# Returning Y by transposes instead of transfers, and a rearranged hand-over to the second stage

## The chip, the cores and the metric

The kernel runs on one core of a Trainium2 chip. Times are device microseconds (us) of that core. A core has TensorE (PE; its weight loads are shown as PEld), VectorE (DVE), ScalarE (ACT), GpSimd (POOL), SyncE (SP) and 16 DMA engines. "Clock" is the share of TensorE's full rate that was granted.

## The reference, cut to what matters

```python
# x: 8 x 3264 x 192; first a causal 7-tap convolution per head (8 heads), giving x again, then:
X = np.fft.rfft(x, axis=1)                     # only the first 64 modes are used
Yr = einsum('bmd,mde->bme', Xr, w_r) - einsum('bmd,mde->bme', Xi, w_i)
Yi = einsum('bmd,mde->bme', Xr, w_i) + einsum('bmd,mde->bme', Xi, w_r)
y = np.fft.irfft(Y, n=S, axis=1)
u = x + y
return u + np.maximum(u @ w_ch, 0.0)           # float32, 8 x 3264 x 192
```

The matrices w_r and w_i (64 of 192 x 192 each) have to be loaded whole. The kernel uses (x + y) @ w_ch = x @ w_ch + G (Y @ w_ch), where G is the inverse transform, so Y is needed in two layouts: transposed (`yeT`) as the weights for Y @ w_ch, and with the modes on the partitions (`zy`) as the moving operand of G Y.

## The kernel before

Modes are worked in 16 groups of four. The parts that matter (cuts marked):

```python
def mix(g):                      # Y of four modes; two groups share one PSUM tile
    ...                          # 12 products per group, waiting for wtiles[g]
    ymix = workp.tile([P, D], BF16, tag="ymix")
    nc.scalar.activation(out=ymix[:], in_=zt[:, 0:D], func=ACT.Copy, ...)
    nc.sync.dma_start(out=zy[16 * i:16 * i + 16, :, :], in_=ymix[:, :])
    return ymix

def mix_t(g, ymix):              # two transposes and a copy make yeT
    ...

for g in range(NGRP):
    m = mix(g)
    ...                          # load of weights for a later group, into a freed buffer
    for _ in range(TPER[g]):     # steps of transposing the x data
        t_next(...)
    if g in (11, 13, 14): prefill()   # x @ w_ch of a unit, ahead of Y
    ...
# hand-over: zw = Y @ w_ch (16 products), then the units
zw_part(0); zw_part(1)
for n in range(4): gz(n)         # z += G zw, then relu on ACT
prefill(); gy(0); gz(4); gy(1); prefill(); gy(2); gz(5); gy(3)   # gy: z += G Y, then VectorE add and store
# then the loop: two half-row tiles (64 rows) of two units run side by side
```

There are 108 units of 128 rows by two batches. A "unit" ends with VectorE's add; two adds make one store. A "bank" is one of the PSUM tiles in which TensorE sums its products. A form such as 64*128 in the lines below gives the rows and columns of the weights; products on 64 rows and products on 128 rows are in different tile modes. `zwps<-ident` are filler products (`keep_warm` in the kernel) whose results are not used.

## Time and profile before

| | before |
|---|---|
| median | 183.28 us (3 runs, 183.02 to 183.29) |
| span of the profiled run | 181.4 us |
| last weight packet / sixteenth mix | 108.77 / 109.36 us |
| P0, the first zw product | 111.07 us |
| P0 to the start of the last G zw product, called "the ramp" with the experiments | 62.84 us |

The last line is read from the instruction records: the first zwps product at 111.07, the last `z<-zw` product of the loop at 173.91 (some `z<-win` and `z<-zy` products follow it, until 175.47). The prediction below shows the page's slices, the chain and the windows. Two more views: first who waited for whom from 56 to 110 us; the columns are total wait, times, longest wait:

```profile
PE yp L454 <- DMA wt<-in_moe_w_i_dram: 4.0, 4, 1.4
...
PE yp L454 <- DMA fst<-in_moe_w_i_dram: 1.6, 1, 1.6
```

Those are the mixes waiting for their weights: 5.6 us in which TensorE could do other work. Then VectorE's timeline at the hand-over (start, length, what, idle before it and what ended that):

```profile
113.98 2.42 DVE L572 TENSOR_TENSOR t<-z,x_all 128x384 f32<-128x384 f32 x5 [0.64 <-issue]
116.63 0.56 DVE L572 TENSOR_TENSOR t<-z,x_all 128x384 f32<-128x384 f32 x1 [0.22 <-PE z L502]
118.73 6.28 DVE L572 TENSOR_TENSOR t<-z,x_all 128x384 f32<-128x384 f32 x11 [1.54 <-PE z L537]
```

VectorE stands idle for 1.54 us before its seventh add.

### The profile page before, as it was taken

The numbers are of one execution on the slowest core, as the hardware profiler recorded it, in microseconds if no ns is written. First come the engines' busy times: TensorE is split into PE (matmuls) and PEld (weight loads), VectorE is DVE, ScalarE is ACT, GpSimd is POOL, SyncE is SP. The second block draws the span as 40 slices with busy tenths as digits, with TensorE's granted clock in tenths as the row PEclk, the third lists the DMA queues.
The fourth block names the chain that finished last, engine by engine and source line by source line (L and its number), as shares of the span: only waits on it lengthen the run. The fifth ranks groups of instructions, "written<-read, shape, count | busy, mean of one in ns | idle before, by whom it ended". The sixth has DMA issues, their size and how long they took to land.

```text
span 181.4 us, 5402 instructions
## 1 busy us (share of the span) xinstructions
PE 147.8 (81%) x2115; PEld 128.9 (71%) x2115; DVE 127.8 (70%) x256; ACT 112.9 (62%) x189; POOL 48.8 (27%) x74
## 2 busy tenths in 40 slices
PE   0373579989889969894649977999999999999970
PEld 0242359978779959783538866699999999999940
DVE  5879986553544446974462554679999999999990
ACT  2353994555558617774444453588888888888850
POOL 7969332459322244432523100000000000000000
PEclk9999558999999999999985999999999999999997
DMA  2999999999999999999999990479999999999995
GB/s 60 247 191 191 192 192 191 193 190 192 193 192 193 204 206 207 206 208 210 203 206 207 207 178 11 150 238 306 345 358 353 349 324 366 348 341 328 326 353 188
DMA packets 66819, 42.37 MB, mean 234 GB/s; under 512 B 30218, under 2 KB 66794, under 8 KB 66794
## 3 DMA queue, kind: packets, MB, share of 16 engines
q0 software_dynamic: 36048, 19.75, 78.2%
q1 hardware_dynamic: 30746, 22.28, 37.5%
q8 instruction: 16, 0.26, 0.7%
q14 instruction: 9, 0.07, 0.1%
HBM read 40.31 MB, written 21.01 MB: 338 GB/s over the span
## 4 chain that ended last, share of the span: by engine, by line
DMA 54%; PE 38%; POOL 2%; issue 2%; DVE 1%; DVEq 0%; ACT 0%; POOLq 0%; ACTq 0%
DMA x_all<-in_x_dram 29%; PE z L520 19%; DMA wt<-in_moe_w_i_dram 19%; PE z L537 13%; DMA fst<-in_moe_w_i_dram 6%; PE tp L418 2%; POOL x_all L61 2%; PE z L502 1%; PE yp L454 1%; PE zwps L488 1%; DVE t L572 1%; PE z L510 0%; POOL wt L251 0%; DVEq L722 0%; ACT ymix L463 0%
## 5 line engine op out<-in xcount | busy, mean ns | idle before, releaser
L572 DVE TENSOR_TENSOR t<-z,x_all 128x384 f32<-128x384 f32 x108 | 59.4, 557 | 3.9 <-PE z L537 1.5
L542 ACT ACTIVATE z<-z 128x384 f32<-128x384 f32 x108 | 50.7, 476 | 11.6 <-PE z L520 1.7
L537 PE MATMUL z<-zy,gst 64*128 64x384 bf16 x204 | 46.1, 323 | 0.2
L520 PE MATMUL z<-zw,gst 64*128 64x384 bf16 x204 | 46.1, 323 | 0.0
L520 PE MATMUL z<-win,cTa 64*128 64x192 bf16 x375 | 40.9, 243 | 0.0
L267 ACT CAST x_all<-cp 122x864 bf16<-122x864 f32 (+2 forms) x34 | 28.7, 880 | 15.4 <-PE cp L260 15.2
L520 PEld LDWEIGHTS <-cTa 64*128 64x128 bf16 x450 | 34.9, 94 | 2.8
L260 PE MATMUL cp<-x_all,cband 128*128 128x192 bf16 (+2 forms) x192 | 25.9, 287 | 8.8 <-DVE x_all L269 4.6
L260 PEld LDWEIGHTS <-cband 128*128 128x128 bf16 x192 | 19.7, 109 | 12.7 <-issue 5.4
L61 POOL DMA_DIRECT2D x_all<-in_x_dram x23 | 22.0, 969 | 10.8 <-DMA x_all<-in_x_dram 8.5
L269 DVE CAST x_all<-cp 122x768 bf16<-122x768 f32 (+2 forms) x14 | 14.7, 1054 | 13.2 <-PE cp L260 13.2
L423 ACT COPY cTa<-tp 128x854 bf16<-128x854 bf16 (+1 forms) x16 | 14.1, 910 | 14.7 <-PE tp L418 14.7
L282 PE MATMUL xp<-x_all,fst 122*128 122x192 bf16 (+1 forms) x216 | 22.0, 251 | 0.9 <-DVE x_all L269 0.5
L282 PEld LDWEIGHTS <-fst 122*128 122x128 bf16 (+1 forms) x216 | 18.2, 99 | 2.1 <-DVE x_all L269 0.7
L520 PEld LDWEIGHTS <-gst 64*128 64x128 bf16 x204 | 18.9, 94 | 0.7 <-issue 0.7
L520 PE MATMUL z<-win,cTb 64*128 64x192 bf16 x135 | 19.2, 243 | 0.0
L422 DVE COPY cTa<-tp 128x854 bf16<-128x854 bf16 (+1 forms) x17 | 10.6, 623 | 10.8 <-PE tp L418 10.6
L520 PE MATMUL z<-wB,cTa 64*128 64x192 bf16 x75 | 18.2, 243 | 0.0
L537 PEld LDWEIGHTS <-gst 64*128 64x128 bf16 x204 | 16.1, 93 | 1.0 <-POOLq L554 0.9
L520 PEld LDWEIGHTS <-cTb 64*128 64x128 bf16 x162 | 14.4, 94 | 1.1
L418 PE MATMUL tp<-ident,x_all 122*128 122x122 bf16 x216 | 15.0, 228 | 0.0
L251 POOL DMA_DIRECT2D wt<-in_moe_w_r_dram x14 | 8.6, 612 | 20.2 <-PE yp L454 6.2
(98 smaller groups left out, 169.5 us busy)
## 6 DMA issues: line engine op xcount, KB each, us to landing
out_dram<-t SPq DMA_DIRECT2D x52, 384.0 KB, 4.1
wt<-in_moe_w_r_dram POOLq DMA_DIRECT2D x14, 288.0 KB, 11.4
wt<-in_moe_w_i_dram POOLq DMA_DIRECT2D x14, 288.0 KB, 11.6
x_all<-in_x_dram POOLq DMA_DIRECT2D x8, 432.0 KB, 12.3
x_all<-in_x_dram POOLq DMA_DIRECT2D x7, 480.0 KB, 13.0
x_all<-in_x_dram POOLq DMA_DIRECT2D x8, 384.0 KB, 14.4
x<-in_x_dram SPq DMA_DIRECT2D x1, 768.0 KB, 6.0
fst<-in_moe_w_r_dram POOLq DMA_DIRECT2D x2, 288.0 KB, 10.5
```

Of the source, the lines that this page charges most:

```text
L61: nc.gpsimd.dma_start(out=x_all[:, b, c0:c0 + n, :], in_=src)
L260: nc.tensor.matmul(cp[:, j, 0:GRP * n].rearrange("p (w e) -> p w e", w=n), cband[:, h, :], x_all[:, b, w0:w0 + n, GRP * h:GRP * h + GRP], ...
L267: nc.scalar.copy(out=dst, in_=srcv)
L269: nc.vector.tensor_copy(out=dst, in_=srcv)
L282: nc.tensor.matmul(xp[:, 0:D], fst[0:k, c, :], x_all[0:k, b, c, :], start=(u == FIRST[b] and c == w0), stop=(u == LAST[b] and c == w0 + n ...
L418: nc.tensor.transpose(tp[:, WIN * k:WIN * k + WIN], slot_lhsT(p, k0 + k), ident[0:WIN, 0:WIN])
L422: nc.vector.tensor_copy(out=got[0][0], in_=got[0][1])
L423: nc.scalar.copy(out=got[1][0], in_=got[1][1])
L520: return nc.tensor.matmul(o, lhsT, rhs, start=start, stop=stop, skip_group_check=True, tile_position=(lo, 0))
L537: return [lambda: nc.tensor.matmul(zp[:, 0:2 * D], gst[lo:hi, WIN * w:WIN * w + P], zwi[(h, 1, k)][lo:hi, :], start=False, stop=(r == 1), ...
L542: return nc.scalar.activation(out=zp[:, 0:2 * D], in_=zp[:, 0:2 * D], func=ACT.Relu)
L572: add = nc.vector.tensor_tensor(out=t[:, 2 * k:2 * k + 2, :], in0=zp[:, 0:2 * D].rearrange("p (i e) -> p i e", i=2), in1=x_all[:, 4 * h + ...
```

## The change

Its intent: take six of the eight zy transfers off DMA engines that are full in the weight phase, by transposing `yeT` back on TensorE; let DVE and ACT copy two banks side by side at the hand-over; do the x product of a fifth unit before Y is there; fill VectorE's hole. Cut to its core:

```diff
+    YPE = 6
-        nc.sync.dma_start(out=zy[16 * i:16 * i + 16, :, :], in_=ymix[:, :])
+        if i >= YPE:
+            nc.sync.dma_start(out=zy[16 * i:16 * i + 16, :, :], in_=ymix[:, :])
+    def y_back(half):
+        tp = pt.tile([P, 1024], BF16, tag="p", name="yb")
+        n = 16 * YPE
+        for i in range(4):
+            for e in range(2):
+                e0 = 64 * e
+                nc.tensor.transpose(tp[0:n, D * i + P * e:D * i + P + 64 * e],
+                                    yeT[e0:P, e, 4 * half + i:n * B:B], ident[e0:P, e0:P])
+        nc.vector.tensor_copy(out=zy[0:n, 4 * half:4 * half + 4, :],
+                              in_=tp[0:n, 0:4 * D].rearrange("p (b e) -> p b e", b=4))
 ...
-    TPER = (1, 2, 1, 2, 2, 2, 1, 1, 2, 1, 2, 1, 2, 1, 1)
+    TPER = (1, 2, 1, 2, 2, 2, 1, 2, 2, 2, 2, 1, 1, 1, 0)
 ...
-            if g in (11, 13, 14):
+            if g in (10, 11, 14):
                 prefill()
+            if g in (12, 13):
+                y_back(g - 12)
 ...                                   # and one prefill more at group 14
-    zw_part(0)
-    zw_part(1)
-    for n in range(4):
-        gz(n)
+    zw_mm(0, 0, zwps[0:2])            # one batch in each of two banks
+    zw_mm(0, 1, zwps[2:3])
+    gz(0)
+    zw_mm(1, 0, zwps[0:1])
+    gz(1)
+    gz(2)
+    gy(0)
+    gz(3)
+    gy(1)
+    gz(4)
+    zw_mm(1, 1, zwps[1:2])
 ...
-    N, NF = len(seq), 6
+    N, NF, NY = len(seq), 6, 8        # units 6 and 7: y product whole, not in halves
```

## The prediction

> **What bounds the kernel now.** I read the page's slices first, then the chain that ended last in order of time, then the windows, then the timelines of TensorE and VectorE around the hand-over. The page:
>
> ```profile
> span 181.4 us, 5402 instructions
> ...
> PE   0373579989889969894649977999999999999970
> ...
> PEclk9999558999999999999985999999999999999997
> DMA  2999999999999999999999990479999999999995
> ...
> zy<-ymix SPq DMA_DIRECT2D x8, 48.0 KB, 5.6
> ```
>
> There are two halves. In slices 2 to 24 the DMA row reads 9 while TensorE has holes; from slice 27 TensorE reads 9 without a break. The chain shows the hand-over between them:
>
> ```profile
> 99.78 9.54 DMA wt<-in_moe_w_i_dram
> 109.32 0.04 issue
> 109.36 0.51 PE yp L454 x12
> ...
> 110.72 0.30 DVE yeT L473
> 111.02 0.05 issue
> 111.07 1.54 PE zwps L488 x16
> ```
>
> So the last weight transfer sets when the sixteenth mix may start (109.36), and 1.71 us later the second-stage products (zwps) start at 111.07; I call that moment P0. The windows show the two bounds:
>
> ```profile
> 86.00:90.00 4.00, 2.60 (x54) 2.33 (x51) 1.32 (x3) 1.30 (x2) 1.90 (x4) 1.00 1.22 207
> ...
> 94.00:98.00 4.00, 3.54 (x41) 3.26 (x41) 1.15 (x2) 0.87 (x1) 1.22 (x2) 0.50 1.21 207
> ...
> 140.00:174.60 34.60, 34.60 (x601) 32.08 (x596) 33.70 (x61) 28.75 (x62) 0.00 (x0) 1.00 1.02 341
> ```
>
> The columns are stretch and length, busy time of PE, weight loads, DVE, ACT and POOL, granted clock, DMA share, GB/s. In the weight phase TensorE has over a microsecond to spare in four and the rate stays at 207 GB/s; in the last stage TensorE is busy for 34.60 of 34.60 us. VectorE's 33.70 looks as full, but its adds start 0.573 us apart there, and only 0.465 apart where they queue (114.46, 114.92, 115.38), so it follows TensorE. TensorE needs 0.573 us for a unit: 0.164 + 3 x 0.082 = 0.41 for the z products of two half-row tiles side by side, and 0.164 for the y products. The end is therefore P0, plus the ramp to the steady pattern, plus a fixed number of 0.573 us periods and a fixed tail.
>
> **What the Trainium skill says.** "DMA: Bandwidth & Descriptors", section "Issuing engines are not separate DMA queues": transfers issued by any engine run on the same 16 DMA engines and interleave. The trace agrees: from 64 to 104 us its packet records start 88.5 weight packets per half microsecond when no zy packet starts in it, and 68.9 when over 40 do. "PSUM — Partial Sum Buffer", "PSUM bank collisions raise a hardware error": guard by bank, not by address. The trace agrees that the kernel does so: the ACT copy of the other batch of one zwps bank waited for the DVE copy (1.78 us idle before it, released by DVE zw L492). "TensorEngine Tiling (Array Packing)", "Key Properties": a change of tiling mode drains TensorE. The timeline agrees, with about 0.1 us:
>
> ```profile
> 114.54 0.33 PE L502 MATMUL z<-zw,gst 128*128 128x384 bf16 x1
> 114.70 0.33 PE L502 MATMUL z<-zy,gst 128*128 128x384 bf16 x1
> 114.96 0.33 PE L520 MATMUL z<-zw,gst 64*128 64x384 bf16 x1
> ...
> 115.30 0.24 PE L520 MATMUL z<-wB,cTa 64*128 64x192 bf16 x1
> 115.47 0.34 PE L502 MATMUL z<-zy,gst 128*128 128x384 bf16 x1
> 115.74 0.33 PE L520 MATMUL z<-zw,gst 64*128 64x384 bf16 x1
> ```
>
> Two 384-column products of one mode start 0.16 apart; from 128 to 64 rows it is 0.26, from 64 back to 128 rows 0.17 against 0.08. "TensorE: Matmul & The Clock Gate", Part 1: TensorE is held at half clock after a window of little activity. The trace agrees that it happens (0.50 above, after the emptier stretch 82 to 94).
>
> **The change, part by part.**
>
> 1. Six zy transfers go. Each is 128 packets of 384 B (with 16 small ones for the semaphore). By the regression over those half microseconds one zy packet displaces 0.32 weight packets, so a transfer costs 128 x 0.32 = 41 packets at 177 per us, 0.23 us. The ends of the weight transfers say the same: 1.43 us apart undisturbed, 1.65 to 1.68 where a zy transfer falls between. All six lie before the last weight packet (108.77), and the queue never starved: at the issue of each of the last ten transfers between 4.0 and 5.2 were outstanding. Gain 6 x 0.23 = **1.4 us** of P0.
>
> 2. In return come 16 transposes and two copies of 96x768. Transposes of this kind start about 0.06 us apart at full clock, the like copy of 128x854 takes 0.60: 0.5 us of TensorE and 0.6 of VectorE in each of groups 12 and 13. The weight transfers come every 3.1 us, and a group there holds a mix (0.5), one transpose step of the x data (0.9) and these. TPER has 22 steps before and after, moved to groups 7 and 9, where TensorE waited 1.41 and 1.55 us ahead of the next mix for a transfer. Group 14 keeps no step. So this hides: **0**.
>
> 3. A fifth unit is prefilled before P0: four products of 0.082, **-0.33 us** after P0.
>
> 4. The second-stage weights. Before, all sixteen products run (1.38 us) and then the first z, so TensorE is full, with one wait of 0.14. After, eight run (0.72); the first batch pair sits in two banks, so DVE and ACT copy side by side. A copy starts 0.28 after the start of its last product and takes 0.36 or 0.32, and TensorE answers 0.08 later: first z at P0 + 0.99 instead of 1.38. But TensorE idles 0.27 for that, then 0.07 for the 0.55 copy of the other pair, then about 0.23 for the second relu (0.48 after its z has ended), since gy(1) comes right behind. About 0.57 of idling against 0.14: **+0.4 us**, and it eats the prefill's gain. What it buys is the first VectorE add 0.6 us earlier, and VectorE is not the bound.
>
> 5. Units 6 and 7 take their y whole. Work is unchanged (two halves side by side or one whole, 0.164; the pairing is one slot longer than its units in both). But each whole y in the loop changes mode twice: 4 x 0.1 = **+0.4 us**. It closes VectorE's hole of 1.54 us ahead of 118.73, which delays nothing on TensorE.
>
> Followed instruction by instruction, the loop's round 12 starts at P0 + 7.4 now and P0 + 7.9 changed; from there both are alike. Sum: -1.4 - 0.33 + 0.4 + 0.4 and roundings, that is -1.4 + 0.5 = **-0.9 us**, so 183.28 - 0.9 = 182.4.
>
> **Rivals.** (a) The transfers were hidden, and the weight phase ends when it did. For it: the DMA share of 1.21 is an overlap of packets, not a proof of a full engine, and the last transfer ended 2.19 us after the one before, so its tail depends on the slowest engine. Against: 1.43 against 1.66. Then only the ramp counts: 183.8. (b) The ramp is free: VectorE's earlier start or banks coming free earlier matter, and the mode changes hide behind waits. For it: the author wrote it to fill VectorE's hole. Against: no wait of TensorE on a bank from 118 on. Then 183.28 - 1.4 - 0.33 = 181.55. (c) TensorE becomes late for the last mix, through the transposes at half clock as in 94 to 100.7. Its slack before mix 15 is 0.62 now and the work of group 14 shrinks, but a half clock that falls on the ramp would cost up to 1.7 us: 183.5 or more. Busier groups 7 and 9 speak against it.
>
> **Range and chances.** The centre takes part 1 whole and the ramp as worked out. The ends come from (b), and from half of part 1 lost or a bad clock window: 181.3 to 183.5. Two per cent is 3.7 us, more than twice all gains together: 0.02 faster, 0.97 the same, 0.01 slower.
>
> **What would show it.** Right for part 1: the sixteenth mix starts near 107.9 to 108.1, and weight transfers end 1.43 apart up to the seventh zy. Part 2: no wait of that mix on a DVE or ACT copy. Part 4: P0 to the first 64-row product about 4.05 us, with TensorE gaps ahead of the first z and of gy(1). Part 5: about 0.1 extra on either side of four whole y products in the loop, and the adds continuous with no hole of 1.5 us, yet still 0.573 apart. Wrong if mix 15 still starts at 109, if the adds run closer than 0.573 apart, or if the clock row has a 5 between the hand-over and the end.

## The result, and the profile after

The changed kernel takes 185.80 us (median of 4 runs, 185.46 to 186.11) beside 183.22 (4 runs, the three above and one more): ratio 1.0142, 95% interval 1.0122 to 1.0162. It is **slower by 1.4%**, clear of noise, though "the same" in the classes of 2% that the chances of the prediction go by. A ratio here is the mean time of one kernel's fast runs over that of the other's fast runs of the same rounds, so it is not quite the ratio of the medians. Executions over 1.5% slower than the fastest of the same kernel are left out of the means. The page of the changed kernel:

```profile
span 184.0 us, 5415 instructions
...
PE   0363679979989878867777989999999999999980
...
PEclk9999559999999999999999756999999999999997
DMA  2999999999999999999999920377999999999996
```

Two things differ from before. The DMA row falls a little earlier, so the weight phase did get shorter. And the low stretch of the clock row has moved, from slices 21 and 22 to slices 23 to 25, onto the hand-over. The chain that ended last, in order of time (start, length, what):

```profile
99.84 0.85 PE tp L418 x14
100.69 2.28 PE yb L477 x8
102.97 0.41 PE yp L455 x12
103.38 1.36 PE tp L418 x14
104.75 2.52 PE yb L477 x8
107.30 0.35 DVE zy L479
108.10 0.71 PE yp L455 x9
108.81 2.03 PE z L525 x12
110.84 0.64 PE zwps L628 x6
111.48 0.64 PE yp L455 x9
```

Before, a weight transfer of 9.54 us stood at this place. Now TensorE's own work, but for one VectorE copy at 107.30, leads to the sixteenth mix (111.41 in the records), nearly four microseconds after the last weight packet (107.49). (zwps of L628 are the fillers; the second-stage products start at P0, now 113.47.) The two groups of eight transposes back (yb) take 2.3 and 2.5 us, not 0.5. The windows name the second part; the first line is the kernel before, the other two the changed one:

```profile
104.00:108.00 4.00, 3.00 (x60) 2.74 (x53) 2.96 (x7) 1.98 (x4) 0.00 (x0) 1.00 1.16 200
104.00:108.00 4.00, 3.59 (x18) 2.73 (x16) 1.31 (x3) 0.87 (x1) 0.00 (x0) 0.50 0.86 150
108.00:112.00 4.00, 3.90 (x42) 3.06 (x41) 0.05 (x1) 0.00 (x0) 0.00 (x0) 0.50 0.00 0
```

The clock of the changed kernel was 0.50 for both stretches; by the clock records from 103.5 to 113.8, a length of 10.24 us. In 104 to 108 TensorE counts as 3.59 us busy with 18 matmuls; before it did 60 in 3.00 us. VectorE afterwards:

```profile
119.22 0.56 DVE L587 TENSOR_TENSOR t<-z,x_all 128x384 f32<-128x384 f32 x1 [0.22 <-PE z L517]
120.83 0.56 DVE L587 TENSOR_TENSOR t<-z,x_all 128x384 f32<-128x384 f32 x1 [1.05 <-PE z L517]
121.62 0.56 DVE L587 TENSOR_TENSOR t<-z,x_all 128x384 f32<-128x384 f32 x1 [0.23 <-PE z L517]
122.90 2.28 DVE L587 TENSOR_TENSOR t<-z,x_all 128x384 f32<-128x384 f32 x4 [0.72 <-PE z L552]
```

The single hole of 1.54 us became three of 1.05, 0.23 and 0.72. The adds then go on 0.573 us apart as before.

### The profile page after: what moved, and what is told of

The parts are those of the page before. It is cut to its first block, busy times and chain, and to the rows that moved or that the text cites. A ratio compares the mean times of both kernels' runs of the same rounds, so it can differ in the third digit from the quotient of the medians.

```text
span 184.0 us, 5415 instructions
## 1 busy us (share of the span) xinstructions
PE 152.4 (83%) x2129; PEld 131.4 (71%) x2129; DVE 127.7 (69%) x258; ACT 112.9 (61%) x188; POOL 49.1 (27%) x74
## 4 chain that ended last, share of the span: by engine, by line
DMA 47%; PE 43%; POOL 3%; issue 2%; DVE 2%; ACT 0%; DVEq 0%; POOLq 0%
DMA x_all<-in_x_dram 30%; PE z L535 19%; DMA wt<-in_moe_w_i_dram 18%; PE z L552 13%; PE yb L477 3%; POOL x_all L61 3%; PE tp L418 2%; PE yp L455 2%; PE z L517 1%; PE z L525 1%; PE zwps L628 1%; DVE t L587 1%; PE zwps L503 1%; POOL wt L251 0%; DVE yeT L487 0%
## 5 line engine op out<-in xcount | busy, mean ns | idle before, releaser
L552 PE MATMUL z<-zy,gst 64*128 64x384 bf16 x200 | 45.2, 323 | 0.2
L260 PE MATMUL cp<-x_all,cband 128*128 128x192 bf16 (+2 forms) x192 | 24.7, 277 | 8.7 <-DVE x_all L312 4.6
L260 PEld LDWEIGHTS <-cband 128*128 128x128 bf16 x192 | 18.8, 106 | 12.2 <-DVE x_all L312 5.5
L535 PEld LDWEIGHTS <-gst 64*128 64x128 bf16 x204 | 18.7, 94 | 1.0 <-issue 1.0
L552 PEld LDWEIGHTS <-gst 64*128 64x128 bf16 x200 | 15.8, 93 | 1.0 <-POOLq L569 0.9
L418 PE MATMUL tp<-ident,x_all 122*128 122x122 bf16 x216 | 13.6, 217 | 0.0
```

The lines of the kernel that those rows point to most:

```text
L260: nc.tensor.matmul(cp[:, j, 0:GRP * n].rearrange("p (w e) -> p w e", w=n), cband[:, h, :], x_all[:, b, w0:w0 + n, GRP * h:GRP * h + GRP], ...
L418: nc.tensor.transpose(tp[:, WIN * k:WIN * k + WIN], slot_lhsT(p, k0 + k), ident[0:WIN, 0:WIN])
L535: return nc.tensor.matmul(o, lhsT, rhs, start=start, stop=stop, skip_group_check=True, tile_position=(lo, 0))
L552: return [lambda: nc.tensor.matmul(zp[:, 0:2 * D], gst[lo:hi, WIN * w:WIN * w + P], zwi[(h, 1, k)][lo:hi, :], start=False, stop=(r == 1), ...
```

## The experiments

Where did the expected gain go? The weights did come earlier, but TensorE was no longer ready for them. Theory A: switching between 128-row and 64-row tiles at every one of the 16 transposes. Rivals: the stride of the weight reads (B), the moved transposes and prefills (C), a weight load of fewer than 128 columns (D, formed after the first runs); and for the size of the loss, the half clock (E). Eleven kernels ran, all correct.

**1. All transposes in one mode** (`e1_one_mode`), the changed kernel with

```diff
-                nc.tensor.transpose(tp[0:n, D * i + P * e:...], yeT[e0:P, e, ...], ident[e0:P, e0:P])
+                nc.tensor.transpose(tp[0:n, D * i + 64 * e:D * i + P + 64 * e],
+                                    yeT[:, e, 4 * half + i:n * B:B], ident[:, :])
```

> The changed kernel with all 16 transposes back in the full 128-row mode (the second of each pair also redoes 64 columns that the first wrote, with the same values). Theory A (what made the change slow is that each of the 16 transposes switches between 128-row and 64-row tiles and then starts 0.29 to 0.34 us after its forerunner): they start 0.06 to 0.1 us apart here, each group of eight takes under 0.8 us instead of 2.4 to 2.65, the sixteenth mix is released by its weight transfer near 108.1 us, no half clock falls on 104 to 114 us, and the time falls by 2.5 to 3.5 us to 182.3 to 183.3. Theory B (the transposes are slow because their weights are read with a stride of 8 elements): they stay near 0.3 us apart and the time stays at 185.8.

Measured: 182.09 us, ratio 0.9928 to before (0.9904 to 0.9952). TensorE's timeline:

```profile
100.45 1.57 PE L476 MATMUL yb<-ident,yeT 128*96 128x128 bf16 x8
...
103.21 1.57 PE L476 MATMUL yb<-ident,yeT 128*96 128x128 bf16 x8
...
107.95 0.48 PE L455 MATMUL yp<-wt,xt 128*32 128x192 bf16 x12 [0.41 <-DMA wt<-in_moe_w_i_dram]
...
109.67 0.47 PE L502 MATMUL zwps<-win,yeT 128*128 128x192 bf16 x3 [0.23 <-DVE yeT L486]
```

The sixteenth mix waits for its weights again, at 107.95, and no half clock falls near it. So the time falls as theory A says, 0.2 us below its range even. But the starts are 0.176 us apart, not the 0.06 to 0.1 expected: the mode is only part of a transpose's cost, and something else makes these transposes slow.

**2. Four of a kind, then the other four** (`e2_grouped`), the two `for` lines of the transposes exchanged.

> The same 16 transposes as in the changed kernel, 128 and 64 rows, but four of one kind and then four of the other, so one switch within a group of eight instead of seven. Theory A: each group of eight takes about 1 us (six starts of 0.06 to 0.1 and one or two switches of 0.3), the time is within 0.5 us of e1. Theory B, or a theory that 64-row transposes are slow by themselves: 64-row ones stay 0.3 apart and the time is over 184.5.

Measured: 183.37, with two runs at 184.2 and 184.4 and two at 181.7 and 182.5; ratio 0.999 (0.9938 to 1.0043). The 64-row transposes start 0.18 apart like the 128-row ones, so they are not slow by themselves, and the one switch in a group costs 0.27 to 0.31 from start to start. The profile happened to be of the slower sort, with half clock from 102.2 to 112.4: transposes hardly slower than in run 1 and a P0 2.4 us later than in run 1 all the same:

```profile
104.15 1.73 PE L477 MATMUL yb<-ident,yeT 128*96 128x128 bf16 x8
...
112.09 0.99 PE L503 MATMUL zwps<-win,yeT 128*128 128x192 bf16 x8
```

It is a miss for the time expected, and the first sign that the half clock is a cause of its own.

**3. No transposes back** (`e3_no_yback`), the changed kernel with YPE = 0 and no y_back.

> The changed kernel with all eight zy transfers by DMA and no transposes back: the prefill, the bank split, the whole y products and the moved transposes alone. Theory A with the ramp as predicted (0.5 to 0.7 us longer than before, because of waits and mode switches): sixteenth mix near 109.3 us as before, time 183.6 to 184.0. Rival (the ramp costs nothing): 182.9 to 183.3. Rival C (the moved transposes and prefill make TensorE late and cause the half clock, not the transposes back): sixteenth mix near 111 us, time over 185.

Measured: 184.57, ratio 1.0063 (1.0036 to 1.0089), somewhat more than expected. From P0 to the last z product it takes 63.35 us against 62.84 before: the ramp costs the 0.51 that was predicted. P0 itself came 0.49 later than before (111.56), with the last weight packet 0.57 later (109.34) and half clock from 106.2 to 109.6; why the packets were later isn't settled. The sixteenth mix started at 109.86, not at 111, so rival C is out as the main cause.

**4. The Y part alone, as in the change** (`e4_yback_alone`), the kernel before with YPE, y_back and the new TPER.

> The kernel before with the Y part alone (48 modes by the transposes of the changed kernel, alternating in mode, and the moved transposes of the x data), with the ramp of before. Theory A: the sixteenth mix is late by 2 to 2.5 us, half clock near 104 to 114 us, time about 185.2. Rival C: if the prefill schedule is what makes TensorE late, the time is about 182.

Measured: 185.60, ratio 1.0102 (1.0059 to 1.0145); sixteenth mix at 112.23, half clock from 101.9 to 112.1, ramp 62.84 as before. The Y part alone brings nearly the whole loss. One of its four runs took 183.81.

**5. The Y part alone, in one mode** (`e5_one_mode_alone`), run 4 with the diff of run 1.

> The kernel before with the Y part alone, its 16 transposes all in 128-row mode. Theory A (the zy transfers cost 1.3 to 1.4 us of the weight phase; the ramp of the change costs 0.5): the transposes start 0.18 us apart as in the one-mode run, the sixteenth mix is released by its weights near 108 us, the hand-over takes as long as before (62.8 us from the first second-stage product to the last z product), time 181.6 to 181.9. Rival (the ramp of the change costs nothing on the whole): 182.1 as in the one-mode run.

Measured: 181.37, ratio 0.9912 (0.9895 to 0.9928). P0 at 109.65 instead of 111.07, the last weight packet at 107.53 instead of 108.77, ramp 62.84. The six transfers were worth 1.2 to 1.4 us, as predicted; the time came 0.2 us below the range expected.

**6. One mode, units 6 and 7 in halves** (`e6_no_whole_y`), run 1 with NY = 6.

> The one-mode run with no whole y product in the loop beyond those of the kernel before (units 6 and 7 in halves). Theory A: four mode switches less, 0.1 us each: 0.4 us faster than the one-mode run, 181.6 to 181.8, and VectorE's hole of about 1.5 us before its seventh add is back. Rival (filling VectorE's hole pays): equal to the one-mode run or slower, 182.1 or more.

Measured: 181.29, ratio 0.9904 (0.9886 to 0.9922). The ramp is 62.93 instead of 63.36, so the two whole y products cost 0.43, four switches of 0.1 each. The time came 0.3 us below the range expected. VectorE's timeline has its hole back, at no cost to the end:

```profile
117.34 8.00 DVE L586 TENSOR_TENSOR t<-z,x_all 128x384 f32<-128x384 f32 x14 [1.54 <-PE z L551]
```

**7. One mode, loads of 128 columns** (`e7_wide_weights`), run 1 with the last 32 columns read and not used (their place is set to zero early on):

```diff
-                                    yeT[:, e, 4 * half + i:n * B:B], ident[:, :])
+                                    yeT[:, e, 4 * half + i:P * B:B], ident[:, :])
```

> The one-mode run with the transposes back reading 128 columns instead of 96 (the last 32 are not used). Theory D (a weight load of under 128 columns is slow, 0.25 to 0.27 us, and that is why the one-mode transposes still start 0.176 us apart): loads of 0.1 to 0.15 us and starts 0.06 to 0.09 apart. Rival (the stride of 8 elements is what makes the load slow): still 0.176. Time within 0.3 us of the one-mode run either way, for there they already hide behind the weight transfers.

Measured: 181.86, ratio 0.9945 (0.9916 to 0.9974). TensorE's timeline:

```profile
100.49 0.67 PE L477 MATMUL yb<-ident,yeT 128*128 128x128 bf16 x8
102.09 0.47 PE L456 MATMUL yp<-wt,xt 128*32 128x192 bf16 x12 [0.94 <-DMA wt<-in_moe_w_i_dram]
```

Eight transposes now take 0.67 us instead of 1.57, starts 0.06 to 0.07 apart; a weight load is recorded with 0.14 to 0.16 us instead of 0.25 to 0.27. The stride is the same, so B is out as the cause by itself: loading 96 columns is slower than loading 128. The stride is not free (loads of 128 adjacent columns, those of the x data, are recorded with 0.098 us at full clock in the profile before), but 128 strided columns do not hold the transposes up. No run loads 96 adjacent columns, so this is shown for strided loads only. This agrees with the Trainium skill, "TensorE: Matmul & The Clock Gate", section "Weight-path perf modes — Fast Weight Load (FWL) and DoubleRow", which says that the fast load is on when the number of weights is 128. TensorE, which was ready in run 1 as well, only waits longer (0.94 us at 102.09), and the time is not told apart from run 1's.

**8. Alternating, loads of 128 columns** (`e8_wide_alternating`), the changed kernel with n replaced by P in the transposes.

> The changed kernel, its transposes alternating between 128 and 64 rows as there, but with loads of 128 columns. It splits the 0.29 to 0.37 us of a start into the slow load and the switch. Theory A+D (both add up): starts 0.17 to 0.23 apart, a group of eight takes 1.3 to 1.8 us, time between the one-mode run and the changed kernel, 182.3 to 184.5. If the switch alone makes the 0.3: starts stay at 0.3 and the time at 185.5 or more. If the load alone: 0.06 to 0.09 and the time of the one-mode run.

Measured: 181.57, ratio 0.9935 (0.9906 to 0.9963), faster than expected and 4.2 us below the changed kernel's median. Starts are 0.16 to 0.21 apart. So at full clock one transpose back takes:

| start to start, us | 128-row only | alternating with 64-row |
|---|---|---|
| loads of 128 columns | 0.06 (run 7) | 0.16 to 0.21 (run 8) |
| loads of 96 columns | 0.176 (run 1) | 0.27 to 0.32 (the change) |

The narrow load adds 0.11, the switch 0.10 to 0.15, and they add up. Taking away either one is enough to have TensorE ready in time.

**9. A fuller ramp** (`e9_ramp_dense`), run 7 with NY = 6 and the second-stage products in whole banks:

```diff
-    zw_mm(0, 0, zwps[0:2])
-    zw_mm(0, 1, zwps[2:3])
+    zw_mm(0, 0, zwps[0:1])
+    zw_mm(0, 1, zwps[1:2])
+    zw_mm(1, 0, zwps[2:3])
     gz(0)
-    zw_mm(1, 0, zwps[0:1])
+    zw_mm(1, 1, zwps[0:1])
 ...                              # then gz(1) gz(2) gz(3) gy(0) gz(4) gy(1) prefill gy(2) gz(5) gy(3)
```

> Toward a version that beats both: one-mode transposes with loads of 128 columns, five units prefilled, units 6 and 7 in halves, and the second-stage products in three whole banks first (12 products), the last four after the first z, so that TensorE waits less than in the bank split. Theory A: first second-stage product to last z product 62.5 us (62.84 before, 62.93 in the run without whole y products), time 180.9 to 181.2. Rival (the ramp does not matter below 62.9): 181.3.

Measured: 181.28, ratio 0.9894 (0.9871 to 0.9918). The ramp is 62.59, about as expected, but the last weight packet of the profiled run came at 107.85, and the time isn't told apart from runs 5 and 6: it is what the rival expected, so a gain from the fuller ramp is not shown.

**10. Seven groups by transposes** (`e10_seven_groups`), run 9 with YPE = 7 and both y_back calls in group 14.

> The same with seven groups of modes (56) returned by transposes, both groups of eight transposes in group 14, one zy transfer left. Theory A: one more zy transfer off the weight phase, 0.2 us: 180.7 to 181.0. Rival (TensorE is late for the sixteenth mix, since all 16 transposes stand in one group): equal to the run before or slower, and the sixteenth mix not released by its weights.

Measured: 183.12 (183.01 without the slow run), five runs from 182.85 to 183.75 and one at 181.00; ratio 0.9973 (0.993 to 1.0016). A miss, and a telling one. TensorE had little to do ahead of it:

```profile
98.00:102.00 4.00, 1.46 (x29) 1.07 (x26) 1.95 (x4) 1.46 (x2) 0.36 (x1) 1.00 1.21 207
102.00:104.00 2.00, 1.44 (x28) 1.15 (x28) 0.85 (x2) 0.90 (x2) 0.00 (x0) 0.94 1.20 207
104.00:108.00 4.00, 2.98 (x33) 2.69 (x34) 0.56 (x1) 0.30 (x1) 0.00 (x0) 0.50 0.78 131
```

The third number is TensorE's busy time: 1.46 of 4 us, then the clock falls to 0.50. Transposes with wide loads in one mode start 0.11 apart there instead of 0.06, prefill products 0.16 instead of 0.08, and the sixteenth mix starts at 110.04 without a wait for its weights (last packet 107.42). No slow transpose is in this kernel; the half clock, with all 16 transposes in the last group, costs about 1.7 us against run 9 in the medians of the fast runs.

**11. More matmuls between the slow transposes** (`e11_more_activity`), the changed kernel with

```diff
+            for _ in range(4):
+                nc.tensor.matmul(tp[:, 768:1024].bitcast(F32), ident[:], ident[:], start=True, stop=True)
```

standing after each pair of transposes. That is 32 matmuls, four after each pair; the text says 64 by mistake. The records show that they add 0.18 us to each pair, 1.45 us in all, so a rival that sees only the added work should have said about 187.2.

> The changed kernel with its slow alternating transposes, and four matmuls of ident by ident (128 columns, result unused) after each of the 16: 64 matmuls more, at full clock some 3.6 us more work for TensorE and 16 of them switching mode where a switch was anyway. Theory E (the half clock from 103.5 to 113.8 us, which the low activity of the slow transposes brings about, is the larger part of the loss): full clock through the hand-over and the time falls or stays, 184.0 to 186, in spite of the added work. Rival (the half clock is by the way, and the slow transposes alone make TensorE late): the added 3.6 us show in full, 188.5 or more.

Measured: 186.13, with two runs at 185.4 and 185.5 and two at 186.8 and 187.0; ratio 1.0145 (1.0107 to 1.0184), beside 1.0142 for the change, just above the range of theory E. The half clock shrank to 3.41 us, from 109.0 to 112.4, and the added work showed by 0.3 us in the median. That leans to theory E, but weakly: the profile is one execution, and the four runs lie on both sides. Runs 2 and 10 say more about it.

**Where the 3.8 us went.** P0 is 113.47 in the changed kernel and 109.67 in run 1, which has the same ramp, prefills and transfers. Run 2 lies between them: its transposes are nearly as fast as those of run 1, but its profile has a half clock of 10.24 us as the changed kernel's, and P0 is 112.09. So, from these three profiles, about 2.4 us of the delay is the half clock and about 1.4 us the slow transposes themselves. (0.35 us of the first part lie after the sixteenth mix: from it to P0 it takes 2.06 us in the changed kernel and in run 2, 1.72 in run 1.) It is an estimate, since the half clock began at 102.2 in one and at 103.5 in the other.

## Why the prediction was wrong, point by point

- **What bounds the kernel**: right. Every run that was not late has the sixteenth mix released by its weights and adds 0.573 us apart to the end.
- **Part 1, six transfers are worth 1.4 us**: right. The last weight packet came 1.28 us earlier in the changed kernel, and P0 1.42 us earlier in run 5, where nothing else stood in the way.
- **Part 2, "Transposes of this kind start about 0.06 us apart at full clock ... So this hides: 0"**: this is the step that failed. The 0.06 fits the transposes of the x data (0.053 us apart in the profile before), which load 128 columns and stay in one mode for a step. The transposes back load 96 columns and change between 128 and 64 rows at each one; they start 0.27 to 0.32 us apart at full clock and up to 0.37 at half. Runs 1, 7 and 8 show that the narrow load and the switch add up to this. The prediction had measured a switch at about 0.1 us a paragraph earlier and used it for part 5, but not here, where the diff shows `e0 = 64 * e` in the inner loop. A group of eight took 2.4 and 2.65 us where 0.5 was put down. With that, the prediction's own list for one group (a mix 0.5, a step 0.9 and these) comes to 3.8 us or more, and the weights come every 3.1 us; so it could not hide, and TensorE's work, not the weights, led to the sixteenth mix.
- **Parts 3 to 5, the ramp 0.5 us longer**: right in the sum, 63.35 or 63.36 against 62.84 us in runs 1, 3, 7 and 8. In run 1 the first z starts 0.95 us after P0 and the first 64-row product 3.98 us, where 0.99 and 4.05 were put down. The whole y products cost 0.43 (run 6), and the bank split eats the fifth prefill: 62.93 against 62.84. That is the +0.4 - 0.33 of the prediction.
- **Rivals**: (c), TensorE late for the last mix through transposes at half clock, is what happened. It was put down to transposes as fast as before and "up to 1.7 us"; the time went to 185.80. The prediction's reason against it, busier groups 7 and 9, bears on an earlier stretch: these groups run from 85 to 94 us. In the changed kernel's profile the half clock of 94 to 100.7 is gone (that the busier groups removed it is not shown; runs 2, 4 and 11 have them too, and a half clock from about 85 to 88.5), and the next one began at 103.5, where it costs. (a) is out by runs 1 and 5. (b) is out by runs 3 and 6.
- **The balance**: P0 2.40 us later and a ramp of 63.46 instead of 62.84 (0.1 of it, against run 1, with the start still at half clock) put the last add at 179.65 instead of 176.63. The span grew by 2.6 and not by 3.0, because the end came 4.32 us after the last add instead of 4.76; why, no run tells (in the other profiles this tail takes 4.1 to 4.8).

What caused the half clock is not shown. In run 10 it came after TensorE had done little for some microseconds, in the changed kernel amid the slow transposes. But run 1, whose transposes are slower than those of run 7, had none in its profile near the hand-over, and run 2 had it in its profile and, by its two sorts of times, seemingly not in all of its runs.

Runs 1, 5, 6, 7, 8 and 9 beat both kernels. The best, runs 5, 6 and 9, lie at 181.3 to 181.4 us, 1% below the kernel before, and are not told apart. The simplest is run 5: the kernel before with the transposes back in one mode, and the ramp left as it was.

## What to carry to other kernels

Take the cost of a new matmul or transpose from one with the same number of weight columns and the same tile mode before and after it, not from one that merely does the same job: here the same transpose took 0.06, 0.18, 0.16 to 0.21 or 0.3 us by these two alone. Work that is to hide in the waits of a phase has to be counted against the waits of the very groups where it stands, and once at half clock as well, for slow transposes and half clock together took 3.8 us of P0, more than twice the gain of 1.4 us. Filling another engine's hole is worth nothing where that engine isn't the bound.

## What the Trainium skill lacked or had wrong

- "TensorE: Matmul & The Clock Gate", section "LDWEIGHTS (loading the stationary operand)", gives columns / 1.2 in ns, so 80 for 96 columns and 107 for 128. The runs show the reverse order: 0.25 to 0.27 us recorded for 96 columns, 0.14 to 0.16 for 128 with the same stride, and starts 0.176 against 0.06 us apart. The section on the fast load, cited at run 7, has the condition of 128 weights and a gain of about twofold as measured; the loads agree with that roughly (0.26 against 0.15 us), but for the starts of these strided transposes missing it cost nearly threefold.
- "TensorEngine Tiling (Array Packing)", section "Key Properties", says that a change of mode drains TensorE, without a figure: 0.1 us between 384-column products, 0.10 to 0.15 us between transposes.
- "TensorE: Matmul & The Clock Gate", section "Why this matters for your kernels", warns of idle gaps over about 3 us between bursts; another part of the page names frequent short idles too, without a length. In run 10 the clock fell to half at 103.75 us, and from 80 us up to there no wait of TensorE was over 1.43 us (waits of 1.18 and 1.43 us ended at 99.31 and 102.07, and one of 1.51 us had begun at 103.5). So staying under 3 us did not keep the full clock; what would have is not shown. The window of about 3.4 us in Part 1 of the page does agree with the lengths: half-clock stretches before the end of the program were 3.41, 6.83, 10.24 or 13.65 us, one to four times 3.41.
